# Windowed attention with sink keys and a gated layer behind it: a new order of the vector engine's work, and the sinks and the bias in groups of 32 rows

## The chip, the cores and the metric

The kernel runs on one core of a Trainium2 chip. Times are device microseconds (us) of one execution. The kernel before takes 119.67 us, the median of 3 runs (118.62 to 120.17).

## The reference, cut to what matters

Four batches of 8 heads, 768 positions, 64 values per head. A query sees the 128 keys up to its own position and the 4 first keys of its batch (the sinks). The heads of a position, side by side, make a row of 512 values, which goes through a gated layer.

```python
scores = scale * np.matmul(q, k.transpose(0, 1, 3, 2))
is_sink = pos[None, :] < int(n_sink)                 # n_sink 4
in_window = (rel >= 0) & (rel < int(window))         # window 128, rel = query - key
scores = np.where(is_sink | in_window, scores, -1000000000.0)
a = np.exp(scores - max); a = a / (np.sum(a) + 1e-09)
x = rows of np.matmul(a, v)                          # 3072 rows of 512
H = np.maximum(x @ w_h, 0.0)
T = 1.0 / (1.0 + np.exp(-(x @ w_t + b_t)))
out = T * H + (1.0 - T) * x
```

## The kernel before, in words

The 3072 rows are 24 tiles of 128, 6 for each batch; n is a tile, t its number in the batch. A tile of keys is seen by the queries of its own tile and of the next one, so `scores(n)` multiplies tile n's keys with the queries of tiles n and n+1 (16 matmuls, 4 heads at a time in 4 groups of 32 rows). A tile goes through these functions:

- TensorE (PE): `scores`, `sink_scores` (for t of 2 and more, where the sinks lie outside the window), `values` (exponentials times V, with a first matmul for the sinks' V in each half), `x_transpose`, `bias` (a row of ones times the bias, which starts the sum), `gate` (times w_t), `hidden` (times w_h).
- ScalarE (ACT): `expo` (exponentials of `scores`, into E), `sink_expo`, `x_copy` (the transposed X out of PSUM), `tanh`, and below tile 16 `gate_on_act` (tanh into the gate's value).
- VectorE (DVE): `mask` (E times a mask of zeros and ones), `norm` (a reciprocal of the sums, then X = values times it), `diff` (max(H,0) - X), `gated` (times the gate), and `transpose_qk` or `transpose_tile`, which transpose 32x32 blocks of the loaded Q and K into `tr`.
- GpSimd (POOL): `finish` (adds X, writes O; SP then stores it), `gate_value` from tile 16 on, `sink_keys`, `sink_values`, and nearly all loads: `load_part` (Q and K of batches 0 to 2, a number of neighbouring rows to a partition), `load_whole` (batch 3), `load_v` and `load_v_heads`.

The order on each engine is the order in which the code is written (`_keep_traced_order`). One pass of the loop over s (lines 552 to 599) works on four tiles at once: scores and exponentials of n2 = s+2, mask, values and X of n1 = s+1, gate and hidden of n0 = s, and diff, gated and finish of n9 = s-1. Below, "step n2" is that pass. The lists `pieces`, `tiles` and `loads` say which transposes and loads belong to a step; a load stands ahead of the step's finish on POOL in `loads[n2][0]`, or behind it in `loads[n2][1]`.

In a step DVE's order is diff(n9), mask(n1), gated(n9), the transposes, norm(n1). PE's order is sink_scores(n2), x_transpose(n0), scores(n2), bias(n0), half of gate(n0), values(n1), the other half of gate(n0), hidden(n0). `ps_v` holds the values of a tile, and its second bank X transposed; `ps_z` holds the sink scores and then the gate's sum.

Ahead of the loop (lines 175 to 550) the first tiles are started while the loads come in. SP loads the bias (`b32`, one row) and the sinks' V (`vs32`, 32 rows: head and sink). `sink_values(b)` spreads `vs32` over a block-diagonal `vs[b]`, in POOL's order behind the first loads and ahead of those of batch 1 (`second`).

Of the kernel before, what the change touches and what calls it, by code (L numbers as in the profile page):

```python
# [32 lines left out]
def kernel(  # L33
# [13 lines left out]
    P = 128  # L47
# [59 lines left out]
    def load_part(b, i, g, which, into=None, engine=pool):  # L107

        t0, nt = segments[b][which][i]
        into = nat[b][which][i] if into is None else into  # L110
        engine.dma_start(  # L111
            out=into[32 * g:32 * g + 32].rearrange("p hg m d -> p hg (m d)"),
            in_=(q, k)[which][b, :, t0:t0 + nt, :].rearrange(
                "(g hg) (r m) d -> g r hg (m d)", g=G, m=nt // 32)[g])

    def load_whole(g, which):
        pool.dma_start(
            out=whole[32 * g:32 * g + 32, which].rearrange("p hg m d -> p (hg m) d"),
            in_=(q, k)[which][B - 1].rearrange(
                "(g hg) (m r) d -> g r (hg m) d", g=G, r=32)[g])  # L120

    def part_loads(b, i, which):

        return [lambda g=g: load_part(b, i, g, which) for g in range(G)]
# [12 lines left out]
    def transpose_tile(n):  # L137

        b, t = divmod(n, NC)
        dst = tr[b].bitcast(FP32).rearrange("p w hg t e -> p (w hg) (t e)")  # L140
        src = whole.bitcast(FP32).rearrange("p w hg m d -> p (w hg) (m d)")
        dve.transpose(out=dst[:, :, t * P:(t + 1) * P], in_=src[:, :, t * P:(t + 1) * P])
# [6 lines left out]
    def load_v_heads(b, h0, h1):  # L149
        pool.dma_start(  # L150
            out=vt[b][0][:, h0:h1].rearrange("p h t e -> p (h t) e")[:, :, 0:D],
            in_=v[b, h0:h1].rearrange("h (t p) d -> p (h t) d", p=P))
# [8 lines left out]
    wt = const.tile([P, KC, DM], FP16, tag="wt")  # L161
    brow = const.tile([P, DM], FP16, tag="brow")
    b32 = const.tile([1, DM], FP32, tag="b32")
    ones = const.tile([P, P], FP16, tag="ones")
    zeros = const.tile([P, H * (D + 1)], FP16, tag="zeros")
    vs32 = const.tile([H * NSINK, B, D + 1], FP32, tag="vs32")
    vmask = const.tile([H * NSINK, H], FP32, tag="vmask")
    skmask = const.tile([P, HG, H], FP16, tag="skmask")
    vs = [const.tile([P, H, D + 1], FP16, tag=f"vs{b}", name=f"vs{b}") for b in range(B)]

    sk = [const.tile([P, HG, 2, P], FP16, tag=f"sk{b}", name=f"sk{b}") for b in range(B)]
# [8 lines left out]
    sp.dma_start(out=b32, in_=moe_b_t.unsqueeze(0))  # L180
    for b in range(B):
        sp.dma_start(out=vs32[:, b, 0:D],
                     in_=v[b, :, 0:NSINK, :])
# [14 lines left out]
    dve.memset(brow, 0.0)  # L198
    dve.memset(skmask, 0.0)
    for g in range(G):  # L200
        for hg in range(HG):
            h = HG * g + hg
            dve.memset(skmask[32 * g:32 * g + 32, hg, h:h + 1], 1.0)
    for tile_v in [tile_v for of_batch in vt for tile_v in of_batch]:
        dve.memset(tile_v[:, :, :, D:D + 1], 1.0)
    dve.memset(vs32[:, :, D:D + 1], 1.0)
    for i in range(2):
        dve.memset(es[i], 0.0)
    dve.memset(sk[0].rearrange("p hg e x -> p (hg e x)"), 0.0)
    dve.memset(vs[0].rearrange("p h e -> p (h e)"), 0.0)  # L210
    for b in range(1, B):
        act.copy(out=vs[b].rearrange("p h e -> p (h e)"), in_=zeros)
        act.copy(out=sk[b].rearrange("p hg e x -> p (hg e x)"), in_=zeros[:, 0:HG * 2 * P])
# [7 lines left out]
    pool.memset(vmask, 1.0)  # L221
    pool.affine_select(out=vmask, in_=vmask, compare_op=ALU.is_ge, fill=0.0, base=0,
                       pattern=[[-NSINK, H]], channel_multiplier=1)
    pool.affine_select(out=vmask, in_=vmask, compare_op=ALU.is_ge, fill=0.0,
                       base=NSINK - 1, pattern=[[NSINK, H]], channel_multiplier=-1)


    def sink_keys(b, engine=pool):
        for hg in range(HG):
            engine.tensor_tensor(  # L230
                out=sk[b][:, hg, :, 0:H * NSINK].rearrange("p e (h s) -> p e h s", s=NSINK),
# [5 lines left out]
    def sink_values(b):  # L237
        pool.tensor_tensor(
            out=vs[b][0:H * NSINK],
            in0=vs32[:, b].unsqueeze(1).to_broadcast([H * NSINK, H, D + 1]),  # L240
            in1=vmask.unsqueeze(2).to_broadcast([H * NSINK, H, D + 1]), op=ALU.mult)
# [12 lines left out]


    def sink_bank(n):
        return (ps_h if n == 3 else ps_z)[:, 0:P]

    def sink_scores(n):
        b, t = divmod(n, NC)  # L260
        first = True
        for hg in range(HG):
            for e in range(2):
                last = hg == HG - 1 and e == 1
                pe.matmul(sink_bank(n),
                          lhsT=sk[b][:, hg, e],
                          rhs=tr[b][:, 0, hg, t * P:(t + 1) * P, e], start=first, stop=last)
                first = False

    def sink_expo(n):  # L270
        nrow = H * NSINK
        act.activation(out=es[n % 2][0:nrow], in_=sink_bank(n)[0:nrow],
                       func=AF.Exp, bias=ebias[0:nrow], scale=SCALE)
# [24 lines left out]

    def values(n):
        b, t = divmod(n, NC)  # L300
        both = av_of(n)
        for i in range(2):
            if t >= 2:
                pe.matmul(both[:, i], lhsT=es[n % 2],
                          rhs=vs[b][:, HB * i:HB * i + HB, :].rearrange("p h e -> p (h e)"),
                          start=True, stop=False, skip_group_check=True)
# [53 lines left out]
    def bias(n, cols=ALL):  # L360
# [313 lines left out]
```

## Time and profile before

| | |
|---|---|
| time, median of 3 runs | 119.67 us (118.62, 119.67, 120.17) |
| the profiled execution | 119.51 us |
| its span, first to last instruction | 117.5 us |
| busy: PE, DVE, ACT, POOL | 86%, 83%, 77%, 73% of the span |
| granted TensorE clock, mean | 0.987 |
| DMA packets | 46160, of which 38594 under 512 B |
| `norm` of tile 8, 14, 22 (second instruction) starts at | 50.70, 75.04, 105.94 us |

Busy shares say how full an engine is over the whole span; the order of starts in the timeline says what a step waits for. An instruction's duration and the distance to the next start differ: on DVE and ACT the next one starts some 0.1 us ahead of the recorded end of the one before. Starts are used for sums.

### The profile page before, as it was taken

What the parts mean: (1) busy time and instruction counts of PE and PEld (TensorE: products, weight loads), DVE (VectorE), ACT (ScalarE), POOL (GpSimd) and SP (SyncE); (2) the same over time, 40 slices, a digit from 0 to 9 for tenths busy, and PEclk for the clock granted to TensorE, in tenths of its full rate; (3) what the DMA queues carried; (4) which work ended last, traced back from release to release, by engine and by line L of the source; (5) the groups of instructions that cost most, each with busy time, mean ns of one, the idle gap of its engine ahead of it and who ended that gap; (6) DMA issues with size and microseconds to landing.
All of it is one profiled execution on the core that took longest, in us unless ns stands there. A gap on an engine that the chain in (4) does not pass through costs nothing.

```text
span 117.5 us, 3064 instructions
## 1 busy us (share of the span) xinstructions
PE 101.4 (86%) x1189; PEld 55.8 (48%) x1189; DVE 97.1 (83%) x186; ACT 91.0 (77%) x116; POOL 85.7 (73%) x118
## 2 busy tenths in 40 slices
PE   5997868599969869799999898999998999999920
PEld 1333445345535435556554454655464556555610
DVE  5589875669995899999998999698889998797580
ACT  0985789659769969899699999798788987964510
POOL 6979997499998997798979999530674336415660
PEclk9999999999999999999999999999999999999995
DMA  3999999989999999999999999999310222022032
GB/s 102 238 204 149 140 144 199 147 116 154 106 153 153 284 280 249 182 169 187 206 213 150 198 164 200 154 196 207 108 72 17 89 95 86 3 95 89 27 150 91
DMA packets 46160, 17.52 MB, mean 149 GB/s; under 512 B 38594, under 2 KB 42434, under 8 KB 46147
## 3 DMA queue, kind: packets, MB, share of 16 engines
q0 software_dynamic: 41744, 9.97, 96.9%
q1 hardware_dynamic: 3938, 6.72, 16.8%
q10 hardware_dynamic: 464, 0.66, 2.2%
q8 instruction: 9, 0.15, 0.5%
q14 instruction: 5, 0.03, 0.1%
HBM read 21.01 MB, written 6.29 MB: 232 GB/s over the span
## 4 chain that ended last, share of the span: by engine, by line
PE 38%; DMA 22%; DVE 21%; issue 8%; POOL 4%; ACT 3%; ACTq 1%; DVEq 0%
PE ps_z L365 10%; DMA wh<-in_moe_w_h_dram 9%; PE ps_h L398 9%; DMA nat<-in_k_dram 5%; DVE DD L402 5%; DMA first<-in_q_dram 5%; DVE E L289 5%; DVE tr L134 4%; PE ps_v L316 4%; PE ps_s L250 3%; DVE X L326 3%; DMA nat<-in_q_dram 3%; PE ps_v L313 2%; DVE DD L406 2%; PE ps_v L353 2%
## 5 line engine op out<-in xcount | busy, mean ns | idle before, releaser
L281 ACT ACTIVATE E<-ps_s,ebias 128x2048 f16<-128x2048 f32 (+1 forms) x24 | 43.7, 1822 | 2.1 <-PE ps_s L250 2.1
L411 POOL TENSOR_TENSOR O<-DD,X 128x512 f32<-128x512 f16 (+1 forms) x24 | 27.1, 1134 | 21.4 <-DVE DD L406 13.1
L365 PE MATMUL ps_z<-wt,XT 128*128 128x512 f16 (+1 forms) x96 | 27.6, 375 | 0.4
L398 PE MATMUL ps_h<-wh,XT 128*128 128x512 f16 (+1 forms) x96 | 24.2, 374 | 1.4 <-DMA wh<-in_moe_w_h_dram 1.4
L289 DVE TENSOR_TENSOR E<-E,mask_std 128x2048 f16<-128x2048 f16 (+1 forms) x20 | 22.8, 1138 | 0.3 <-ACT E L281 0.2
L134 DVE STREAM_TRANSPOSE tr<-nat 128x512 f32<-128x512 f32 (+1 forms) x22 | 19.0, 909 | 2.1 <-DMA nat<-in_q_dram 1.1
L402 DVE SCALAR_TENSOR_TENSOR DD<-ps_h,X 128x512 f16<-128x512 f32 (+1 forms) x24 | 16.2, 677 | 4.3 <-PE ps_h L398 3.5
L382 ACT ACTIVATE TH<-ps_z 128x512 f16<-128x512 f32 (+1 forms) x24 | 14.1, 586 | 5.3 <-PE ps_z L365 4.9
L358 ACT COPY XT<-ps_v 128x512 f16<-128x512 f16 x23 | 13.1, 571 | 5.5 <-PE ps_v L353 5.4
L316 PE MATMUL ps_v<-v,E 128*128 128x65 f16 x184 | 15.4, 195 | 1.8 <-DVE E L289 1.5
L326 DVE TENSOR_TENSOR X<-ps_v,rec 128x512 f16<-128x512 f32 x23 | 15.9, 692 | 0.9
L250 PE MATMUL ps_s<-tr 32*128 32x256 f16 (+1 forms) x384 | 14.3, 264 | 1.5 <-DVE mask L492 0.9
L398 PEld LDWEIGHTS <-XT 128*128 128x128 f16 x100 | 9.7, 98 | 11.8 <-issue 1.5
L316 PEld LDWEIGHTS <-E 128*128 128x128 f16 x192 | 12.2, 97 | 6.4 <-DVE E L289 5.1
L313 PE MATMUL ps_v<-v,E 128*128 128x65 f16 x152 | 15.0, 193 | 0.1
L111 POOL DMA_DIRECT2D nat<-in_k_dram x24 | 13.4, 571 | 0.6 <-DMA nat<-in_k_dram 0.6
L313 PEld LDWEIGHTS <-E 128*128 128x128 f16 x160 | 12.5, 98 | 2.3 <-issue 0.2
L111 POOL DMA_DIRECT2D nat<-in_q_dram x20 | 11.2, 564 | 2.2 <-DMA wh<-in_moe_w_h_dram 1.5
L353 PE MATMUL ps_v<-ident,X 128*128 128x128 f16 x92 | 9.0, 220 | 4.2 <-DVE X L326 4.0
L388 ACT ACTIVATE TH<-TH,half 128x512 f16<-128x512 f16 (+1 forms) x17 | 12.0, 709 | 0.5
L191 PE MATMUL ps_h<-zeros 128*128 128x512 f16 x36 | 10.4, 444 | 1.3 <-DVE zeros L194 1.3
L406 DVE TENSOR_TENSOR DD<-DD,TH 128x512 f16<-128x512 f16 (+1 forms) x24 | 10.4, 433 | 0.5 <-POOL TH L393 0.3
(75 smaller groups left out, 131.2 us busy)
## 6 DMA issues: line engine op xcount, KB each, us to landing
out_dram<-O SPq DMA_DIRECT2D x23, 256.0 KB, 5.1
nat<-in_q_dram POOLq DMA_DIRECT2D x16, 96.0 KB, 6.6
nat<-in_k_dram POOLq DMA_DIRECT2D x16, 96.0 KB, 5.5
v<-in_v_dram POOLq DMA_DIRECT2D x4, 384.0 KB, 9.4
v<-in_v_dram POOLq DMA_DIRECT2D x6, 128.0 KB, 5.3
v<-in_v_dram POOLq DMA_DIRECT2D x1, 768.0 KB, 10.8
whole<-in_q_dram POOLq DMA_DIRECT2D x4, 192.0 KB, 6.4
whole<-in_k_dram POOLq DMA_DIRECT2D x4, 192.0 KB, 7.8
```

Source lines behind the costliest of these rows:

```text
L111: engine.dma_start(out=into[32 * g:32 * g + 32].rearrange("p hg m d -> p hg (m d)"), in_=(q, k)[which][b, :, t0:t0 + nt, :].rearrange("(g ...
L134: dve.transpose(out=dst[:, :, lo:hi, :], in_=nat[b][which][i].bitcast(FP32)[:, :, lo:hi, :])
L250: pe.matmul(ps_s[:, g, hg, 0:nq * P], lhsT=tr[b][rows, 1, hg, c * P:(c + 1) * P, e], rhs=tr[b][rows, 0, hg, c * P:(c + nq) * P, e], start= ...
L281: act.activation(out=E[n][:, :, :, 0:nq * P], in_=ps_s[:, :, :, 0:nq * P], func=AF.Exp, bias=ebias, scale=SCALE)
L289: return dve.tensor_tensor(out=e3, in0=e3, in1=m[:, 0:nq * P].unsqueeze(1).to_broadcast([P, H, nq * P]), op=ALU.mult)
L313: pe.matmul(slot, lhsT=E[n - 1][:, g, hg, P:2 * P], rhs=v_of(n - 1)[:, h, :], start=first, stop=False, skip_group_check=True)
L316: pe.matmul(slot, lhsT=E[n][:, g, hg, 0:P], rhs=v_of(n)[:, h, :], start=first, stop=True, skip_group_check=True)
L326: dve.tensor_tensor(out=X[n], in0=av[:, :, :, 0:D], in1=rec.unsqueeze(3).to_broadcast([P, 2, HB, D]), op=ALU.mult)
L365: pe.matmul(z_of(n, cols), lhsT=XT[n][:, kc * P:(kc + 1) * P], rhs=wt[:, kc, cols], start=False, stop=(kc == KC - 1))
L398: pe.matmul(h_of(n, cols), lhsT=XT[n][:, kc * P:(kc + 1) * P], rhs=wh[:, kc, cols], start=(kc == 0), stop=(kc == KC - 1))
L402: dve.scalar_tensor_tensor(out=DD[n][:, cols], in0=h_of(n, cols), scalar=0.0, in1=flat(X[n])[:, cols], op0=ALU.max, op1=ALU.subtract)
L411: ins = pool.tensor_tensor(out=O[n][:, cols], in0=DD[n][:, cols], in1=flat(X[n])[:, cols], op=ALU.add)
```

## The change

Six things are changed.

1. **DVE's order in a step** is mask(n1), diff(n9), gated(n9), norm(n1), transposes. Loads of step 9 and later that stood behind the finish now stand ahead of it, and the first load of a step waits for the step's mask (`behind`).
2. **Sink scores once a batch.** `sinks(b)` runs at t = 2 for tiles 2 to 5 together: 16 matmuls of 32 columns, tile 2+i into partitions 32i to 32i+31 of `ps_z`, and one exponential over 128 partitions in place of four over 32.
3. **Groups of 32 rows.** The sinks' V of a tile are multiplied from 32 rows of `es` and `vs` (`values_of_sinks`), and stand ahead of `gate`, right behind `bias`, which takes one row of another group. For that `vs32` is needed on all 128 partitions: after its four loads SP copies it within SBUF to partitions 32 to 63, and that to 64 to 127. The bias is loaded four times, to rows 0, 32, 64 and 96. The fills with zeros ahead of the loop change with it: six copies on ACT and four memsets on DVE go, others come.
4. **Batch 3 in runs of 2.** `load_whole` takes two neighbouring rows of Q or K (512 B) where it took one (256 B). `transpose_tiles` transposes Q or K of two tiles at a time, writing every second element, in place of Q and K of one tile written densely; there are six such transposes, in steps 15 to 20 rather than 16 to 21.
5. **Loads.** V of tile 4 is issued among the loads of batch 1, ahead of its K, V of tile 5 right behind them. The loads of batches 2 and 3 are spread otherwise over steps 7 to 16.
6. The wait in `finish` becomes the helper `behind`, with no change in what it does.

```diff
-    def load_whole(g, which):
-        pool.dma_start(
-            out=whole[32 * g:32 * g + 32, which].rearrange("p hg m d -> p (hg m) d"),
+    def load_whole(g, which, after=None):
+        behind(pool.dma_start(
+            out=whole[32 * g:32 * g + 32, which].rearrange("p hg (m a) d -> p (hg m) (a d)",
+                                                           a=2),
             in_=(q, k)[which][B - 1].rearrange(
-                "(g hg) (m r) d -> g r (hg m) d", g=G, r=32)[g])
+                "(g hg) (m r a) d -> g r (hg m) (a d)", g=G, r=32, a=2)[g]), after)
...
+    def transpose_tiles(which, t0, t1):
+        dst = tr[B - 1].bitcast(FP32).rearrange("p w hg t e -> p w hg (t e)")[:, which]
+        src = whole.bitcast(FP32)[:, which]
+        dve.transpose(
+            out=dst[:, :, t0 * P:t1 * P].rearrange("p hg (m r a) -> p hg m a r", r=32, a=2),
+            in_=src[:, :, 4 * t0:4 * t1].rearrange("p hg (m a) d -> p hg m a d", a=2))
...
+    for i in range(G):
+        dve.memset(ones_g[32 * i:32 * i + 1, :], 1.0)
+    dve.memset(b32, 0.0)
+    for i in range(G):
+        sp.dma_start(out=b32[32 * i:32 * i + 1, :], in_=moe_b_t.unsqueeze(0))
...
+    dve.memset(vs32.rearrange("p b e -> p (b e)"), 0.0)
...
+    dve.memset(sk.rearrange("p b hg e x -> p (b hg e x)"), 0.0)
+    for b in range(B):
+        sp.dma_start(out=vs32[0:H * NSINK, b, 0:D], in_=v[b, :, 0:NSINK, :])
+    sp.dma_start(out=vs32[32:64], in_=vs32[0:32])
+    sp.dma_start(out=vs32[64:128], in_=vs32[0:64])
...
+    def sink_scores(b):
         first = True
         for hg in range(HG):
             for e in range(2):
+                for i in range(G):
+                    t = 2 + i
+                    pe.matmul(ps_z[32 * i:32 * i + 32, 0:P], lhsT=sk[:, b, hg, e],
+                              rhs=tr[b][:, 0, hg, t * P:(t + 1) * P, e],
+                              start=first, stop=(hg == HG - 1 and e == 1))
                 first = False
...
+    def values_of_sinks(n):
+        b, t = divmod(n, NC)
+        if t >= 2:
+            rows = slice(32 * (t - 2), 32 * (t - 1))
+            for i in range(2):
+                pe.matmul(av_of(n)[:, i], lhsT=es[b % 2][rows],
+                          rhs=vs[b][rows, HB * i:HB * i + HB, :].rearrange("p h e -> p (h e)"),
+                          start=True, stop=False, skip_group_check=True)
...
-    tiles = {n: [n + 2] for n in range(RUNS * NC - 2, N - 2)}
+    tiles = {n: [] for n in range(N)}
+    tiles.update({15: [(0, 0, 2)], 16: [(0, 2, 4)], 17: [(1, 0, 2)], 18: [(0, 4, 6)],
+                  19: [(1, 2, 4)], 20: [(1, 4, 6)]})
...
-    put(segment_loads(2, 0), ((6, 1, 2), (7, 1, 5), (8, 1, 1)))
-    put(v_halves(2), ((8, 1, 1), (9, 1, 1)))
-    put(segment_loads(2, 1), ((8, 1, 1), (9, 1, 2), (10, 1, 5)))
-    put([lambda which=which, g=g: load_whole(g, which)
-         for which in range(2) for g in range(G)], ((11, 1, 3), (12, 1, 3), (13, 1, 2)))
-    put(v_halves(3), ((13, 1, 1), (14, 1, 1)))
+    put(segment_loads(2, 0), ((6, 1, 2), (7, 1, 4), (8, 1, 2)))
+    put(v_halves(2), ((8, 1, 1), (9, 0, 1)))
+    put(segment_loads(2, 1), ((9, 0, 2), (10, 0, 3), (11, 0, 3)))
+    put([lambda after=None, which=which, g=g: load_whole(g, which, after)
+         for which in range(2) for g in range(G)], ((11, 0, 1), (12, 0, 2), (13, 0, 2),
+                                                    (14, 0, 3)))
+    put(v_halves(3), ((15, 0, 1), (16, 0, 1)))
...
     second = segment_loads(1, 0)
+    second.insert(4, lambda: load_v(4))
+    second.append(lambda: load_v(5))
...
         if n2 > 4:
-            if n2 % NC >= 2:
-                sink_scores(n2)
-                sink_expo(n2)
+            if n2 % NC == 2:
+                sinks(n2 // NC)
             x_transpose(n0)
             x_copy(n0)
             scores(n2)
-        bias(n0)
-        if n2 > 4:
+            bias(n0, group=(n1 % NC + 1) % G)
+            values_of_sinks(n1)
             expo(n2)
+        else:
+            bias(n0)
         gate_value(n9)
+        masked = mask(n1) if n2 > 4 else None
         diff(n9)
...
-        else:
-            mask(n1)
         last = gated(n9)
-        for load in loads[n2][0]:
-            load()
+        for i, load in enumerate(loads[n2][0]):
+            load(after=masked if i == 0 else None)
         for n in finished.get(n2, (n9,)):
             finish(n, after=last if n2 < 7 else None)
         for load in loads[n2][1]:
             load()
         if n2 > 4:
+            outputs(n0)
+            gate(n0, parts=range(0, 2))
+            values(n1)
+            norm(n1)
             for piece in pieces[n2]:
                 transpose_qk(*piece)
-        for n in tiles.get(n2, ()):
-            transpose_tile(n)
+        for part in tiles[n2]:
+            transpose_tiles(*part)
         if n2 >= NC and n2 % NC == 0:
             sink_keys(n2 // NC)
         if n2 == N - 1:
             finish(n9, after=mask(n2))
-        if n2 > 4:
-            outputs(n0)
-            gate(n0, parts=range(0, 2))
-            values(n1)
-            norm(n1)
```

## The prediction

> **What bounds the kernel now.** I read the page first: span, busy shares, the row of DMA. The profiled execution took 119.51 us, 1.99 around its span of 117.52; the median is 119.67, so sums against the one hold for the other within 0.2.
>
> ```profile
> span 117.5 us, 3064 instructions
> PE 101.4 (86%) x1189; PEld 55.8 (48%) x1189; DVE 97.1 (83%) x186; ACT 91.0 (77%) x116; POOL 85.7 (73%) x118
> DMA  3999999989999999999999999999310222022032
> ```
>
> No engine stands out, and DMA is full for 28 of 40 slices. So I went on to the timeline of single steps. PE in step 21 (sink scores first):
>
> ```profile
> 94.76 0.39 PE L265 MATMUL ps_z<-tr,sk 128*128 128x128 f16 x4
> 94.99 0.39 PE L353 MATMUL ps_v<-ident,X 128*128 128x128 f16 x4
> 95.31 0.63 PE L250 MATMUL ps_s<-tr 32*128 32x256 f16 x16
> 95.88 0.39 PE L361 MATMUL ps_z<-brow,ones 128*128 128x512 f16 x1
> 96.10 0.59 PE L365 MATMUL ps_z<-wt,XT 128*128 128x512 f16 x2
> 96.53 0.27 PE L304 MATMUL ps_v<-vs,es 128*128 128x260 f16 x1
> 97.43 0.59 PE L365 MATMUL ps_z<-wt,XT 128*128 128x512 f16 x2
> 97.86 1.03 PE L398 MATMUL ps_h<-wh,XT 128*128 128x512 f16 x4
> ```
>
> From start to start: sinks 0.23, transposes 0.32, scores 0.57, bias 0.22, gate 0.43, values 0.90 (of it 0.22 for two sinks' V, and 0.16 in which the second matmul waits for the mask), gate 0.43, hidden 0.91: 4.01 in all. DVE, with three marks of the stages and two waits:
>
> ```profile
> 50.70 0.69 DVE L326 TENSOR_TENSOR X<-ps_v,rec 128x512 f16<-128x512 f32 x1
> ...
> 71.81 1.70 DVE L289 TENSOR_TENSOR E<-E,mask_std 128x2048 f16<-128x2048 f16 x1
> ...
> 75.04 0.69 DVE L326 TENSOR_TENSOR X<-ps_v,rec 128x512 f16<-128x512 f32 x1
> ...
> 94.96 0.69 DVE L402 SCALAR_TENSOR_TENSOR DD<-ps_h,X 128x512 f16<-128x512 f32 x1 [0.26 <-PE ps_h L398]
> 95.57 1.22 DVE L289 TENSOR_TENSOR E<-E,mask_std 128x2048 f16<-128x2048 f16 x1
> 96.70 0.42 DVE L406 TENSOR_TENSOR DD<-DD,TH 128x512 f16<-128x512 f16 x1
> 97.04 0.70 DVE L142 STREAM_TRANSPOSE tr<-whole 128x512 f32<-128x512 f32 x1
> 97.70 0.21 DVE L325 RECIPROCAL rec<-ps_v 128x8 f32<-128x8 f32 x1
> 97.94 0.69 DVE L326 TENSOR_TENSOR X<-ps_v,rec 128x512 f16<-128x512 f32 x1
> 98.92 0.69 DVE L402 SCALAR_TENSOR_TENSOR DD<-ps_h,X 128x512 f16<-128x512 f32 x1 [0.29 <-PE ps_h L398]
> ...
> 105.94 0.69 DVE L326 TENSOR_TENSOR X<-ps_v,rec 128x512 f16<-128x512 f32 x1
> ```
>
> DVE needs 0.61 for diff, 1.13 mask, 0.34 gated, 0.66 transpose, 0.93 reciprocal and X: 3.67, and then waits 0.29 for `hidden`. With the transposes of batches 1 and 2 (0.93 from start to start, as at 53.59) it needs 3.83 to 3.94 and hardly waits. ACT, below tile 16, needs 0.25 for a sink exponential, 0.47 copy, 1.9 expo, 0.63 tanh, 0.63 gate: 3.9. So three engines stand within 0.2 of each other, each behind the others' ends; PE is longest at the end, DVE in the middle. To 45 us the loads decide: K of batch 1 lands at 45.15, its transpose starts at 45.27.
>
> **Part by part.** Marks: X of tiles 8, 14 and 22.
>
> *Sink scores.* ACT loses 12 of 16 small exponentials, 3.0 us. For 16 matmuls of 32 columns there is no row. Between 0.22 (four at a time, 4 x 0.055, the spacing at L265) and 0.88 (one by one) I take the spacing of the 32-row scores, 0.57/16, so 0.57 for 4 x 0.23: PE gains 0.35 a batch. The exponential now stands only in steps 8, 14 and 20; but there PE begins with `sinks`, which needs all queries of the batch: in step 8, those transposed last in step 7.
>
> *Bias and sinks' V.* If two groups of rows run beside each other as scores do, 0.22 goes in each step with t of 2 and more; between 0 and 0.22 I take 0.22, since 16 scores of 256 columns end in 0.57, and one by one, at half of a 512-column bias each, would need 1.76. PE's step falls from 4.01 to 4.01 - 0.23 - 0.22 - 0.16 = 3.40.
>
> *Mask first, X ahead of the transposes.* No work goes; the mask no longer stands behind diff, which waits for `hidden`, and X comes 0.66 to 0.93 earlier in DVE's turn. What is late next is the transposes: keys transposed last in steps 8, 11, 14, 17 and 19 are wanted by PE's scores at the head of the next step. With PE at 3.40 and DVE at 3.83 PE can give that 0.4 a step. So a step costs what DVE needs.
>
> *To tile 8.* I put the new order on the rows from 37.78 on. Step 7: mask 6 at once (E ready at 37.30), diff at 38.9, X at 39.9 rather than 42.32, queries' transposes 41.0 to 42.5. Step 8: sinks behind them, PE's transposes of X at 43.1 (before, behind X's end at 43.0); X of tile 7 at 45.4, key transposes 46.2 to 47.7. Step 9: X of tile 8 at 50.0. Gain **0.7**.
>
> *Tiles 8 to 14.* Five steps at 3.83 and one with half a mask (0.60 for 1.13) at 3.3: 22.5 where 24.34 were. Against it POOL: in steps 9 to 14 two to four loads now stand between mask and finish, 0.54 each for Q and K (L111), 1.43 for half of V, 0.93 for `whole`. The finish (1.15) is clear of the next mask if the loads need less than 3.83 - 1.25 - 1.15 = 1.43. Steps 9 (2.5), 11 (2.5) and 14 (2.8) are over that by an us. What such a meeting costs is the 1.70 at 71.81, beside this finish:
>
> ```profile
> 71.25 1.17 POOL L411 TENSOR_TENSOR O<-DD,X 128x512 f32<-128x512 f16 x1
> ```
>
> It is 0.48 over the usual 1.22 for 0.61 beside each other. Between 0 and 1.15 a meeting I take this row: 3 x 0.48 = 1.4. Gain 24.34 - 22.5 - 1.4 = **0.4**. The Trainium skill (SBUF — State Buffer, section "Who interferes with whom") says that a VectorE instruction with two SBUF inputs and a GpSimd one that reads SBUF shut each other out for the whole instruction, whoever issues first. By that the three meetings would be some 1.0 each, an estimate, this gain -1.2 and the time 118.4; the mechanism stands below as rival C, from rows.
>
> *Tiles 14 to 22.* The transposes of batch 3 write every second element: between 0.66 (L142, dense) and 0.93 (L134, every eighth or twelfth); by the step I take nearer the first, 0.75. A step with one needs 3.76, less 0.06 of reciprocal that no longer waits: 3.70; one with half a mask, or none to transpose, goes with PE at 3.4. X 15 to 22: 5 x 3.70 + 3 x 3.4 = 28.7, and 0.5 for `gate_value` (0.62), which can now meet the mask in steps 19 to 23, for one row like 71.81. 29.2 where 30.90 were: gain **1.7**. At 0.66 it is 2.1, at 0.93 it is 0.8.
>
> *Loads.* V of tile 4 goes 2.1 us forward on POOL, K of batch 1 0.9 back; that K (29.02 now) is wanted behind X of tile 4, at 32. `whole` in 512 B rows halves 12288 packets; K of batch 3, ready 0.6 ahead of use now (77.20, 77.80), is wanted one step later. No gain taken.
>
> *Ahead of the loop.* DVE's fills grow by 0.65 us and end near 4.95; the first K cast waits until 5.28. ACT's six copies (4.10 to 7.3) go, but it waits for Q until 7.74. `vs32` is the danger: by the trace's DMA semaphores its four loads, issued from 4.22 on, were complete at 9.79 to 11.02. They now stand behind four bias rows (a queue's DMA starts behind the landing of its eighth predecessor: Q at 18.55 behind wt's 18.27), so issue from 6.4 to 9.3 and land near 12.8; then two copies, one behind the other. Each between 2.0 (a store at 90.90) and 5.6 (the first vs32 load): `vs32` at 16.8 to 24; I take 3.2 each, 19. POOL reaches `sink_values(0)` at 15.61 and would idle, with the loads of batch 1 behind it; but its third waits until 22.68 for wh's landing, and V of tile 3 lands at 24.86. Cost 0.0 to 0.3, in the 0.7 above already.
>
> *Tail.* Behind X 22 nothing moves but 32-row sinks' V, which here have no bias beside them: +0.1.
>
> **Sum:** 119.5 - 0.7 - 0.4 - 1.7 + 0.1 = **116.8**.
>
> **Rivals.**
>
> *A. More of it.* No meetings, transposes dense (0.66): 116.8 - 1.4 - 0.4 = 115.0. For it: only one mask of 20 now shows a long meeting. Against: the finish moved toward the mask.
>
> *B. The row groups don't run side by side.* Bias and sinks' V cost what they did, `sinks` 0.88; PE at 3.7 decides where DVE had 3.4 (tiles 17, 21, 22) and eats the slack of the others: +0.3 x 3, +0.05 x 10: 118.2. For it: one matmul with one row isn't a score. The Trainium skill (TensorEngine Tiling (Array Packing), section "Key Properties") says a change of tiling mode drains TensorE; the row is XT ahead of scores, 0.32 where four matmuls of 128 columns take 0.23. The change adds two such changes a batch.
>
> *C. POOL and DVE in lockstep.* The mask waits for the finish, the finish for the loads, the loads for the mask: a step lasts 1.25 + loads + 1.15. Steps 9, 10, 11, 12 (with sink_keys 0.55), 13, 14: 4.9, 4.0, 4.9, 4.3, 4.3, 5.2 for 3.83 (12: 3.3), so 5.1 over, where I count 1.4: 120.5. It decides from loads of 1.43 on. Against: if the mask starts first, the finish waits instead, and nothing behind that is urgent.
>
> *D. `vs32` too late* (the slower side). Two copies at 5.6 give 24. Then sinks' values to 26.7, four Q loads to 29.9, landing at 31.9 rather than 26.53; DVE's transpose at 26.66 waits, with all behind it: +5.4 on the forecast, 122.2. Slower than before from an arrival at about 21.5 on. Against: small transfers of 8 KB landed 0.2 to 0.6 apart.
>
> **How the numbers follow.** Forecast 0.40 (own range 115.8 to 117.9), A 0.30, B 0.10, C 0.11, D 0.09. A measurement of this kernel tells about 2% from no change: 117.3 and 122.1. Faster: A, three quarters of the forecast and a little of B: 0.61. Slower: half of D and a tail of C: 0.08. Same: 0.31. The range reaches from A's lower part, 114.2, to where C and D begin to be left out, 120.3.
>
> **What would show it.** Right: in step 21 of the new profile no wait of L316 for the mask, bias and sinks' V within 0.3 together, DVE without a wait for `hidden`; X of tile 8 near 50, tile 14 near 74, tile 22 near 103. Transposes of `whole` near 0.8. Wrong: masks of 1.7 and more in steps 10 to 15 (C), a POOL gap over 4 us ahead of the first `sink_values` (D), bias and sinks' V 0.44 apart (B), DVE waiting for nat or whole (then the loads pace the kernel, and none of the sums hold).

## The result, and the profile after

The change made the kernel **slower**: a median of 128.67 us (127.64 to 129.20, 4 runs) against 119.15 us (118.56 to 120.17, 4 runs) of the kernel before on the same chip, a ratio of 1.078 (95% interval 1.067 to 1.089). That is 11.9 us more than the forecast of 116.8. Ratios here, also below, leave out executions that took over 1.5% more than the fastest of the same kernel, so a median can stand a little off its ratio.

The page of the changed kernel first: the span, what each engine did in it, and the DMA engines' share in 40 slices.

```profile
span 125.9 us, 3063 instructions
...
PE 100.4 (80%) x1189; PEld 50.5 (40%) x1189; DVE 104.2 (83%) x189; ACT 85.4 (68%) x98; POOL 88.5 (70%) x118
...
DMA  3999999136999999999999999989932012220242
```

ACT lost 5.6 us of work, as meant, and DVE gained 7.1, which nobody meant. In the row of DMA there is a hole at slices 8 and 9 (22 to 28 us) that the kernel before doesn't have. Line numbers are now those of the changed kernel: L303 is the mask, L423 diff, L427 gated, L344 and L345 the reciprocal and X, L144 and L151 the transposes, L254 the sinks' values, L432 the finish, L414 `gate_value`, L318 the sinks' V on PE.

The hole has its cause in the chain of work that ended last (start, us, what). Two copies of `vs32` from SBUF to SBUF stand in it, one behind the other:

```profile
11.78 6.93 DMA vs<-vs
18.73 4.81 DMA vs<-vs
```

The timelines of POOL and of DVE (start, length, engine, line, operation, idle time before it and its releaser) show who waits for them:

```profile
23.77 2.08 POOL L254 TENSOR_TENSOR vs<-vs,vmask 128x520 f16<-128x520 f32 x2 [8.17 <-DMA vs<-vs]
...
26.57 0.21 DVE L344 RECIPROCAL rec<-ps_v 128x8 f32<-128x8 f32 x1 [6.81 <-PE ps_v L335]
```

POOL stands 8.17 us at `sink_values(0)`, with the loads of Q of batch 1 queued behind it (they land at 28.5 to 31.4 where they landed at 25.1 to 26.5). PE needs these values for tile 2, and DVE waits 6.81 for PE. X of tile 2 starts at 26.82 rather than 21.34.

The loop has another loss. Two steps on DVE, and POOL's finishes in the same time:

```profile
79.00 1.80 DVE L303 TENSOR_TENSOR E<-E,mask_std 128x2048 f16<-128x2048 f16 x1
80.72 0.68 DVE L423 SCALAR_TENSOR_TENSOR DD<-ps_h,X 128x512 f16<-128x512 f32 x1
81.50 0.43 DVE L427 TENSOR_TENSOR DD<-DD,TH 128x512 f16<-128x512 f16 x1
81.84 0.20 DVE L344 RECIPROCAL rec<-ps_v 128x8 f32<-128x8 f32 x1
82.08 0.69 DVE L345 TENSOR_TENSOR X<-ps_v,rec 128x512 f16<-128x512 f32 x1
82.69 0.70 DVE L151 STREAM_TRANSPOSE tr<-whole 128x512 f32<-128x512 f32 x1
83.31 2.04 DVE L303 TENSOR_TENSOR E<-E,mask_std 128x2048 f16<-128x2048 f16 x1
```

```profile
78.53 1.17 POOL L432 TENSOR_TENSOR O<-DD,X 128x512 f32<-128x512 f16 x1
...
83.09 1.17 POOL L432 TENSOR_TENSOR O<-DD,X 128x512 f32<-128x512 f16 x1
```

Each of these masks begins while a finish runs. The finishes end at 79.70 and 84.26, the masks at 80.80 and 85.35: 1.10 and 1.09 behind the finish. A mask that meets a running finish thus ends as if it did nothing until POOL is done and then took its 1.09. And diff (80.72) to gated (81.50) is 0.78 from start to start, though diff lasts 0.68: in the steps shown of before, diff to mask was 0.61 and mask to gated 1.13, with no gap. The groups of instructions (busy us, mean ns of one, idle before them) have both losses in sum:

```profile
L303 DVE TENSOR_TENSOR E<-E,mask_std 128x2048 f16<-128x2048 f16 (+1 forms) x20 | 27.9, 1396 | 0.2 <-ACT E L295 0.2
...
L427 DVE TENSOR_TENSOR DD<-DD,TH 128x512 f16<-128x512 f16 (+1 forms) x24 | 10.6, 442 | 2.6 <-POOL TH L414 0.5
```

The same two groups before:

```profile
L289 DVE TENSOR_TENSOR E<-E,mask_std 128x2048 f16<-128x2048 f16 (+1 forms) x20 | 22.8, 1138 | 0.3 <-ACT E L281 0.2
...
L406 DVE TENSOR_TENSOR DD<-DD,TH 128x512 f16<-128x512 f16 (+1 forms) x24 | 10.4, 433 | 0.5 <-POOL TH L393 0.3
```

### The profile page after: what moved, and what is told of

It reads as the page before. It is cut to its first block, busy times and chain, and to the rows that moved or that the text cites. A ratio compares the mean times of both kernels' runs of the same rounds, so it can differ in the third digit from the quotient of the medians.

```text
span 125.9 us, 3063 instructions
## 1 busy us (share of the span) xinstructions
PE 100.4 (80%) x1189; PEld 50.5 (40%) x1189; DVE 104.2 (83%) x189; ACT 85.4 (68%) x98; POOL 88.5 (70%) x118
## 4 chain that ended last, share of the span: by engine, by line
DVE 29%; PE 28%; ACT 14%; DMA 12%; issue 10%; POOL 3%; SPq 1%; DVEq 0%; POOLq 0%; ACTq 0%
DVE E L303 11%; DMA vs<-vs 9%; PE ps_z L386 7%; DVE tr L144 6%; ACT E L295 6%; PE ps_h L419 6%; PE ps_v L335 4%; PE ps_s L265 3%; ACT TH L403 3%; DVE X L345 3%; ACT XT L377 3%; DMA vs<-in_v_dram 2%; PE ps_v L332 2%; DVE DD L423 2%; ACT TH L409 2%
## 5 line engine op out<-in xcount | busy, mean ns | idle before, releaser
L432 POOL TENSOR_TENSOR O<-DD,X 128x512 f32<-128x512 f16 (+1 forms) x24 | 28.3, 1181 | 16.2 <-DVE DD L427 8.1
L303 DVE TENSOR_TENSOR E<-E,mask_std 128x2048 f16<-128x2048 f16 (+1 forms) x20 | 27.9, 1396 | 0.2 <-ACT E L295 0.2
L419 PE MATMUL ps_h<-wh,XT 128*128 128x512 f16 (+1 forms) x96 | 25.1, 385 | 0.0
L144 DVE STREAM_TRANSPOSE tr<-nat 128x512 f32<-128x512 f32 (+1 forms) x22 | 18.9, 904 | 0.6 <-DMA nat<-in_q_dram 0.4
L423 DVE SCALAR_TENSOR_TENSOR DD<-ps_h,X 128x512 f16<-128x512 f32 (+1 forms) x24 | 16.0, 665 | 1.0 <-PE ps_h L419 1.0
L345 DVE TENSOR_TENSOR X<-ps_v,rec 128x512 f16<-128x512 f32 x23 | 15.9, 691 | 0.8
L335 PE MATMUL ps_v<-v,E 128*128 128x65 f16 x184 | 14.1, 197 | 2.2 <-DVE E L303 1.8
L335 PEld LDWEIGHTS <-E 128*128 128x128 f16 x192 | 12.1, 98 | 7.6 <-DVE E L303 6.5
L332 PE MATMUL ps_v<-v,E 128*128 128x65 f16 x152 | 13.4, 196 | 0.1
L332 PEld LDWEIGHTS <-E 128*128 128x128 f16 x160 | 11.6, 100 | 3.0 <-issue 1.1
L427 DVE TENSOR_TENSOR DD<-DD,TH 128x512 f16<-128x512 f16 (+1 forms) x24 | 10.6, 442 | 2.6 <-POOL TH L414 0.5
L344 DVE RECIPROCAL rec<-ps_v 128x8 f32<-128x8 f32 x23 | 4.6, 201 | 9.4 <-PE ps_v L335 9.1
L265 PEld LDWEIGHTS <-tr 32*128 32x128 f16 x384 | 7.5, 93 | 11.3 <-DVE tr L144 6.0
```

Source lines behind the costliest of these rows:

```text
L144: dve.transpose(out=dst[:, :, lo:hi, :], in_=nat[b][which][i].bitcast(FP32)[:, :, lo:hi, :])
L265: pe.matmul(ps_s[:, g, hg, 0:nq * P], lhsT=tr[b][rows, 1, hg, c * P:(c + 1) * P, e], rhs=tr[b][rows, 0, hg, c * P:(c + nq) * P, e], start= ...
L303: return dve.tensor_tensor(out=e3, in0=e3, in1=m[:, 0:nq * P].unsqueeze(1).to_broadcast([P, H, nq * P]), op=ALU.mult)
L332: pe.matmul(slot, lhsT=E[n - 1][:, g, hg, P:2 * P], rhs=v_of(n - 1)[:, h, :], start=first, stop=False, skip_group_check=True)
L335: pe.matmul(slot, lhsT=E[n][:, g, hg, 0:P], rhs=v_of(n)[:, h, :], start=first, stop=True, skip_group_check=True)
L345: dve.tensor_tensor(out=X[n], in0=av[:, :, :, 0:D], in1=rec.unsqueeze(3).to_broadcast([P, 2, HB, D]), op=ALU.mult)
```

## The experiments

The theory after this comparison: three losses, namely the copies (4 to 5 us), the order with the mask first (the gap of 0.17 in each step, and more meetings), and the finish behind the loads. Each was undone alone, then all three. In each diff `-` is the changed kernel.

**Straight loads.**

```
-    for b in range(B):
-        sp.dma_start(out=vs32[0:H * NSINK, b, 0:D], in_=v[b, :, 0:NSINK, :])
-    sp.dma_start(out=vs32[32:64], in_=vs32[0:32])
-    sp.dma_start(out=vs32[64:128], in_=vs32[0:64])
+    for b in range(B):
+        for i in range(G):
+            sp.dma_start(out=vs32[32 * i:32 * i + 32, b, 0:D], in_=v[b, :, 0:NSINK, :])
```

> Sink values of V loaded from DRAM straight into all four groups of 32 partitions, 16 small loads on SP and no copy from SBUF to SBUF; all else as changed. Theory (the two copies, 6.93 and 4.81 us, hold POOL at sink_values(0) for 8.17 us, and the loads of batch 1 behind it are late, which costs some 4 to 5 us at tile 2 and is never given back): X of tile 2 starts near 21.5 for 26.82, POOL's wait ahead of L254 falls from 8.2 to under 3, and the time falls by 4 to 5, to 123 to 125. Rival 1 (the late stretch is absorbed later, because the loads of the next batches decide the steps to tile 8 anyway): X of tile 2 comes earlier, X of tile 8 does not, the time stays within 1 us of 128.7. Rival 2 (the chain is the whole loss): the time falls to 119 or below.

Measured: median 125.43, ratio 1.045 (1.034 to 1.057), which is 3.3% less than the change, or some 4 us. POOL's wait is 2.0. But X of tile 2 starts at 24.38, not 21.5, and the two timelines name what took the place of the stall (line numbers are one lower here; the profiled execution is the longest of the four, 126.14):

```profile
14.99 2.67 DVE L302 TENSOR_TENSOR E<-E,mask_std 128x2048 f16<-128x2048 f16 x1
...
15.49 1.08 POOL L253 TENSOR_TENSOR vs<-vs,vmask 128x520 f16<-128x520 f32 x1
```

The mask of tile 1 took 2.67 for 1.22 and again ended 1.09 behind POOL's product (16.57); with all three edits (below) it took 2.71 at the same place. PE's granted clock was down as well, to 0.52 and 0.62 in the stretches from 20 to 24 us. The theory's place was right; the time just missed its 123 to 125, as a second wait appeared.

**Mask second.**

```
-        masked = mask(n1) if n2 > 4 else None
         diff(n9)
+        masked = mask(n1) if n2 > 4 else None
```

> In the steps of the loop the mask stands between diff and gated again, as before the change; all else as changed. Theory (with nothing between them, gated waits for the end of diff, 0.78 from start to start where diff to mask and mask to gated leave no gap, about 0.17 a step in 19 steps; and the mask, going first, stands more often beside POOL's finish, sink_keys and gate_value): the masks' mean falls from 1396 ns to under 1300, the time falls by 3 to 6, to 123 to 126. Rival (mask first is a gain as forecast, since the mask doesn't stand behind hidden, and the losses come from elsewhere): the time rises by 1 to 2 us, steps of the end go from 3.64 back to 4.0.

Measured: 129.13, ratio 1.082 (1.072 to 1.092): no gain. This part of the theory fell. The masks did get shorter (mean 1224 ns) and the gap closed (idle ahead of gated 0.5), but the time came back in front of the reciprocal, which in the changed kernel had 9.4 us of idle time ahead of it:

```profile
L344 DVE RECIPROCAL rec<-ps_v 128x8 f32<-128x8 f32 x23 | 4.7, 206 | 17.9 <-PE ps_v L335 16.4 <-ACT E L295 0.9 <-ACT TH L409 0.6
```

With X ahead of the transposes nothing but gated stands between the mask's end and X, and PE's values, which need the mask, aren't done by then. In this order X first is only to be had with the mask first.

**Finish first.**

```
-        for i, load in enumerate(loads[n2][0]):
-            load(after=masked if i == 0 else None)
         for n in finished.get(n2, (n9,)):
             finish(n, after=last if n2 < 7 else None)
-        for load in loads[n2][1]:
+        for load in loads[n2][0] + loads[n2][1]:
             load()
```

> The finish goes ahead of all loads of its step on POOL, and no load waits for the mask; all else as changed. Theory (in the steps of tiles 8 to 14 the loads push the finish beside the next mask, masks of 1.88, 1.80 and 2.04 us for 1.21): tiles 8 to 14 take about 24 for 26.18 and the time falls by 2 to 3, to 126; the masks beside gate_value and the slow sink_keys stay. Rival 1 (the masks are long because they come first, whichever of POOL's instructions is beside them): the meetings move to other steps, masks' mean within 50 ns of 1396, time within 1 us of 128.7. Rival 2 (lockstep is the whole loss in the middle): the time falls by 4 or more.

Measured: 125.22, ratio 1.048 (1.038 to 1.057), 3.0% better than the change; masks' mean 1214 ns. Tiles 8 to 14 took 24.24 for 26.18, as expected, and tiles 14 to 22 took 30.77 for 31.75. From tile 9 on the masks of the changed kernel are 5.3 us longer than they need, in ten of them; here 1.9, all in tiles 17 to 22. The rival (they are long because they come first) falls.

**All three.** The three edits above together.

> All three edits together: straight loads of the sinks' V, mask between diff and gated, finish ahead of the loads. Theory (chain, order of the mask and late finish are the three losses, about 4.5, 4 and 1.5 with the last two overlapping): 117 to 119.5, level with the kernel before. Rival (something else in the change costs as well, transposes behind X or the sinks at the head of PE's turn): 121 or more.

Measured: 125.53, ratio 1.049 (1.043 to 1.056). The rival held in time. Mask second showed a likely reason: it costs what it gives, and with the finish first there are fewer long masks for it to shorten. In the profile tiles 8 to 14 take 25.75 where finish first alone has 24.24, and X of tile 2 is at 25.40, behind the mask of 2.71 and with a granted clock of 0.50 to 0.52 from 18 to 24 us.

**The beginning mended.** Straight loads, finish first, mask first, and the sinks' values of batches 0 and 1 on DVE, behind masks 1 and 2.

```
+    sink_values(0, engine=dve)      # ahead of norm(1)
...
+    sink_values(1, engine=dve)      # ahead of norm(2)
```

> As the kernel with straight loads of the sinks' V, and with the finish ahead of the loads; besides, the sinks' values of batches 0 and 1 are made by DVE, in its waits ahead of X of tiles 1 and 2, and not by POOL beside mask 1, which took 2.67 us there with straight loads alone. Theory (the start costs 5.4 us at tile 8 in two parts, the copies and POOL's 128-row product beside the mask, and the late finish 2.5 to 3.4 in the loop; nothing else is large): mask 1 at 1.22, X of tile 2 near 21.9, X of tile 8 near 51.0, the loop as with the finish first (24.2 for tiles 8 to 14, 30.8 from there to 22), time 119.5 to 120.5, level with the kernel before. Rival (something else in the first 25 us is late as well, the sinks' scores of all tiles at the head of PE's turn or the clock): X of tile 2 at 23 or later, time over 121.5.

Measured: 122.87, ratio 1.025 (1.016 to 1.033). Mask 1 is 1.22, but X of tile 2 comes at 23.71: the rival. In this profile PE's granted clock was down to 0.6 and 0.7 in the two slices from 18 to 24 us. The next two kernels have the same beginning and a clock of 1.00 there, and X of tile 2 at 22.71 and 22.63: so about 1.0 of the delay goes with the clock, and 1.3 is there without it.

**Three orders.** On that beginning, first the gap covered (the transposes go from behind X to between diff and gated), with POOL kept off the masks:

```
         masked = mask(n1) if n2 > 4 else None
         diff(n9)
+        if n2 > 4:
+            for piece in pieces[n2]:
+                transpose_qk(*piece)
+        for part in tiles[n2]:
+            transpose_tiles(*part)
...
-        for n in finished.get(n2, (n9,)):
-            finish(n, after=last if n2 < 7 else None)
+        for n in finished.get(n2, (n9 - 1,)):
+            finish(n, after=last if n2 < 7 else masked)
...
-        return n < 16 or n == N - 1       # on_act
+        return True
```

> As the kernel with the mended start, but a step's transposes stand between diff and gated, X comes behind gated, the finish of a tile waits for the next step's mask, and the gate's half-and-shift is on ACT for all tiles. Theory (between diff and gated DVE stands 0.17 when nothing is put there; the masks are long only beside POOL's work): a step with 0.93 of transposes goes from 4.02 to 3.85, masks' mean under 1200, tiles 8 to 14 in 23.3, tiles 14 to 22 in 29.5, time 117 to 118.5. Rival (PE or ACT take over at 3.7 to 3.9 a step, or the finish beside diff and transposes makes these longer): 119 to 121.

Measured: 120.42 for the profiled execution and 122.48 to 123.00 for the other three, a median of 122.63 without an interval; so the time decides nothing here beyond that the 117 to 118.5 of the theory was not reached. In the one profile, tiles 8 to 14 took 22.59 and 14 to 22 30.02, the first better than expected, the second worse. But X of tile 7 took 6.46: the sink scores of tile 8 waited 2.7 us for `sink_keys(1)`, which the late finishes of tiles 0 to 3 had pushed back on POOL.

Then, on the same beginning, DVE's order of the kernel before (diff, mask, gated, transposes, X):

> As the kernel with the mended start, but DVE's order in a step is that of the kernel before: diff, mask, gated, transposes, X. So of the change only sink scores at once, the groups of 32 rows, the last batch's runs of 2 and the loads are left. Theory (DVE's turn needs 3.87 again, as before, and bounds the step; PE's and ACT's savings are cover): the loop as before, 24.3 and 30.9, time within 1 us of 119.7. Rival (PE's 0.35 and 0.22 a step and ACT's 3 us come through, since hidden is done earlier and diff waits less): 117 to 118.5.

Measured: 119.55, ratio 0.999 (0.995 to 1.004). The theory held in the time; the loop took 23.36 and 30.74, an us better than before in its first part, and the beginning had X of tile 2 1.3 late. Sink scores at once, the groups of rows, the runs of 2 and the later loads together are worth nothing that shows in the time, although they take 5 us from ACT and some work out of PE's step. The theory's reason, that DVE's own turn bounds the step, fits tiles 8 to 14, but not the end: from tile 14 on diff still waits 0.24 to 0.36 for `hidden` in most steps. There a step is a ring through two engines: mask at 79.83, the first matmul of values that needs it at 81.10, the second half of gate at 81.58, `hidden` at 82.01, diff at 83.14, and the next mask at 83.75, 3.92 later. The sink scores, the bias and the sinks' V stand outside that ring, so what they save doesn't shorten this step.

And the other way round, the kernel before with the mask ahead of diff alone:

> The kernel before with the mask ahead of diff and nothing else of the change; X stays behind the transposes. Theory (0.17 more between diff and gated in some 19 steps, against up to 0.29 of waiting for hidden that goes in the steps of the end; the masks meet gate_value more often): between 119.5 and 122.5, no gain. Rival (the mask first is the gain that was forecast): 118 or less.

Measured: 119.98, ratio 1.002 (0.997 to 1.006). Diff's wait for `hidden` falls from 3.5 us to 1.0, and the gap ahead of gated grows from 0.5 to 2.6; masks' mean goes from 1138 to 1249. What mask first gives, it takes.

**Both orders.** The old order up to X of tile 7, the covered one behind it; then the same with `gate_value` left on POOL.

> The mended start; to the step that makes X of tile 7 DVE's order of the kernel before, with the finish in its place; from there on mask, diff, transposes, gated, X, with the finish behind the next step's mask and the gate's half-and-shift on ACT for all tiles. Theory (the order mask first is worth something once the gap behind diff is filled and POOL is kept off the masks: the covered kernel needed 52.6 us from X of tile 8 to X of tile 22 where the kernel before needs 55.2, and the old order has X of tile 8 at 50.9): X of tile 22 at 103.5, time 116.5 to 117.8, faster than both kernels. Rival (the covered loop only caught up on slack that its late start left in loads and ACT): X 8 to 22 in 54 or more, time 118.5 to 120.

> As the kernel with both, but the gate's half-and-shift of tiles 16 to 22 stays on POOL, where it meets the masks of the last steps. Theory (a meeting costs DVE at least what POOL's instruction lasts): masks of 1.4 to 1.6 in the last steps, 0.5 to 1.5 us slower than the kernel with both, 117.5 to 119. Rival (PE bounds the last steps at 3.65, so that long masks there are hidden): within 0.3 us of it or faster.

Measured: 119.58, ratio 0.998 (0.992 to 1.003), and 119.28, 1.001 (0.997 to 1.004). The time that the theory expected, faster than both kernels, did not come. The loop is as the theory had it: X of tile 8 to X of tile 22 in 52.77 where the kernel before needs 55.24. It was lost ahead of the loop: X of tile 2 at 23.82 for 21.34, with the granted clock again at 0.50 from 20 to 22 us. With the gate on POOL the masks are longer (mean 1182 for 1109 ns) and the same stretch takes 53.44, yet the times don't differ: there the theory of 0.5 to 1.5 us more was not borne out.

**The beginning once more.** The sinks' values of batch 0 behind mask 2 and of batch 1 behind the first gated product, in waits of DVE; with and without four idle matmuls on PE.

```
-    sink_values(0, engine=dve)      # ahead of norm(1)
     norm(1)
+    keep_warm(4)                    # in the first of the two kernels only
...
+    sink_values(0, engine=dve)      # behind mask(2)
     values_of_sinks(2)
     values(2)
-    sink_values(1, engine=dve)
...
     gated(0)
+    sink_values(1, engine=dve)
```

> As the kernel with both, but sinks' values of batch 0 are made behind mask 2 and those of batch 1 behind the first gated product, so that X of tiles 1 and 2 doesn't wait for them; and four idle matmuls (0.2 us each) stand on PE behind the values of tile 1, where the kernel before has the sink scores of tile 3. Theory (the start is late by 1.1 to 1.5 at tile 8 because of 0.4 of sinks' values ahead of X 1, and because PE, idle for 1.5 to 2 us at 17, gets half its clock from 18 to 23): clock at 1.00 from 18 to 24, X of tile 2 at 21.8 to 22.2, X of tile 8 at 50.9, X of tile 22 at 103.6, time 117.0 to 118.2, faster than before by 1 to 2 us. Rival (the dip comes whatever PE does there, or the loads of batch 1 set X of tile 8): X of tile 8 at 51.5 or later, 119.

> The same without the four idle matmuls. Theory (the granted clock falls when PE has been idle there): clock at 0.5 in some 2 us between 18 and 24, X of tile 2 1 to 1.5 later than with them, time 0.3 to 1.3 more. Rival (the wait is only that of sinks' values, which are moved): no difference between the two.

Measured: 118.08, ratio **0.989 (0.984 to 0.994)**, and 118.84, 0.988 (0.982 to 0.995). Both are about 1.1% faster than the kernel before, a small gain, but its interval lies clear of 1. X of tile 2 is at 21.30 and 21.54, X of tile 8 at 50.79 in the first. The idle matmuls made no difference, and the clock was at 1.00 from 16 to 30 us with them and without: that part of the theory fell. How much of the gain is the new place of the sinks' values, and how much a clock that didn't fall in these two profiles, isn't separated. A step of the first one on DVE has no gap and no long mask:

```profile
51.39 1.22 DVE L302 TENSOR_TENSOR E<-E,mask_std 128x2048 f16<-128x2048 f16 x1
52.53 0.69 DVE L422 SCALAR_TENSOR_TENSOR DD<-ps_h,X 128x512 f16<-128x512 f32 x1
53.13 1.09 DVE L144 STREAM_TRANSPOSE tr<-nat 128x512 f32<-128x512 f32 x1
54.06 0.41 DVE L426 TENSOR_TENSOR DD<-DD,TH 128x512 f16<-128x512 f16 x1
54.39 0.19 DVE L343 RECIPROCAL rec<-ps_v 128x8 f32<-128x8 f32 x1
54.62 0.69 DVE L344 TENSOR_TENSOR X<-ps_v,rec 128x512 f16<-128x512 f32 x1
55.22 1.22 DVE L302 TENSOR_TENSOR E<-E,mask_std 128x2048 f16<-128x2048 f16 x1
```

From mask to mask it is 3.83, the very figure that the forecast had for the changed kernel, where its steps from tile 9 to 14 took 4.01 to 4.70.

**The price of the beginning.** The mended loop with the changed kernel's beginning put back, first whole, then with straight loads.

> The best kernel so far (the idle matmuls behind tile 1), but with the whole beginning of the changed kernel put back: the sinks' V copied twice from SBUF to SBUF, their values made on POOL ahead of the loads of batch 1, no idle matmuls. The loop stays mended. Theory (the beginning alone costs 4 to 5.3 us, and none of it comes back, since DVE bounds every later step): X of tile 8 near 55.5 to 56, time 122 to 123.5. Rival (the loop makes up for a late beginning, as its loads are then ahead of need): 120.5 or less.

> The same with the sinks' V loaded straight from DRAM, values still on POOL, where the first product of 128 rows stands beside mask 1. Theory (of the beginning's cost the copies are 2.5 to 3, and POOL's product beside the mask and the idle PE behind it are the other 2): mask 1 at 2.6, X of tile 8 near 52.5 to 53.5, time 119.5 to 121. Rival (the copies are the whole cost): X of tile 8 at 51, time 118.

Measured: 123.36, ratio 1.035 (1.029 to 1.041), and 119.50, 0.992 (0.985 to 1.000). The two differ by the copies alone: 4.3% of the kernel before, 5.1 us, by the two intervals about 1 more or less. Hardly any of it comes back: with the whole old beginning X of tile 8 is 6.4 behind the best kernel's (57.15 for 50.79), X of tile 22 still 5.8 (109.80 for 104.03). The first theory held in the time, though X of tile 8 came an us later than it had. The second had the copies at only 2.5 to 3; its rival, that they are the whole cost, comes closer, since in time the rest can't be told from nothing (0.992 against 0.989), though the profile with straight loads has X of tile 8 at 52.45. The mask of tile 1 took 1.22 this time and POOL's product beside it was the longer one (1.39 for 1.05), but the mask of tile 2 (18.88) met the next product (18.79, 1.05 long) and took 2.05.

## Why the prediction was wrong

By its own marks, in the traces (us; the best is the kernel with the four idle matmuls):

| | before | forecast | changed | finish first | best |
|---|---|---|---|---|---|
| to X of tile 8 | 50.70 | 50.0 | 55.90 | 56.08 | 50.79 |
| X 8 to X 14 | 24.34 | 23.94 | 26.18 | 24.24 | 23.24 |
| X 14 to X 22 | 30.90 | 29.2 | 31.75 | 30.77 | 30.00 |

*To tile 8: missed by 5.9, the largest term.* The step that failed is "I take 3.2 each, 19" for the two copies. They took 6.93 and 4.81, where the same sentence named 5.6 as the upper bound of one, and `vs32` was whole at 23.54, inside its range of 16.8 to 24. So "Cost 0.0 to 0.3" was 5.1 by the last two experiments. The argument against rival D, that small transfers landed 0.2 to 0.6 apart, spoke of loads side by side, and these two stand one behind the other. D's mechanism and price were near the mark: four loads of Q held up behind POOL landed by 31.44 (it had 31.9), the transpose of 26.66 started at 31.56, and the 5.4 was 5.1. It didn't have the other wait, which comes first: DVE stands 6.81 at X of tile 2 for PE's values. The one arrival seen lies beyond D's point of decision of 21.5, which is all that can be said of it. Its chance of 0.09 rested on the argument that fails; the upper third of the forecast's own range for `vs32` was already beyond that point. Both signs that were named for C and D came: a POOL gap of 8.17, and masks of 1.88 and 1.80 in steps 11 and 15.

*Tiles 8 to 14: missed by 2.24.* "3 x 0.48 = 1.4" for meetings: they cost 2.3 by the masks' lengths. The count of three was right, the price was not: the masks of tiles 10, 11 and 14 were 0.66, 0.99 and 0.58 longer. The mask at 71.81 of before follows the same rule (its finish ended at 72.42, the mask 1.09 later), but a meeting costs about what is left of the finish when the mask starts, and that was 0.61 there and 0.70 to 1.10 here. One of the three wasn't where it was forecast: the finish of step 9, beside the mask at 57.44, took 2.21, and the next one, so delayed, met the mask of tile 10: in part rival C, whose lockstep I had argued away with "the finish waits instead". About 1.0 is the gap of 0.17 in six steps, which no step of the prediction has: it summed starts of another order, in which the mask covers what gated waits for. Some 0.3 is left, of it 0.18 in a longer gated beside that late finish.

*Tiles 14 to 22: missed by 2.55.* `gate_value` and `sink_values(3)` and the finishes together lengthened seven masks by some 3.1 us where 0.5 stood; the gap takes 1.4 more. Against it, the transposes in runs of 2 go at 0.62 from start to start, where dense ones took 0.63 to 0.66 before and I took 0.75: 0.8 on the good side. That comes to 3.2, 0.65 more than the miss. By the starts the difference lies in the three steps that the forecast gave to PE at 3.4 (X of tiles 17, 21 and 22): DVE had slack there, and part of its longer work went into it.

*What was right.* `hidden` no longer holds DVE up. ACT's load fell by more than the 3.0 counted. Of the 16 matmuls of 32 columns, 15 took 0.34 (48.54 to 48.88) where I took 0.57 for all. The groups of rows do run side by side, against rival B; PE in a step with sinks' V:

```profile
66.53 0.64 PE L265 MATMUL ps_s<-tr 32*128 32x256 f16 x16 [0.60 <-DVE tr L144]
67.00 0.38 PE L382 MATMUL ps_z<-brow,ones_g 1*128 1x512 f16 x1
67.01 0.38 PE L318 MATMUL ps_v<-vs,es 32*128 32x260 f16 x2
67.32 0.60 PE L386 MATMUL ps_z<-wt,XT 128*128 128x512 f16 x2
```

Bias and sinks' V start 0.01 apart, and from scores to gate it is 0.79 where 0.57 + 0.22 + 0.22 = 1.01 stood: the 0.22 forecast. But this is so in four of the eleven such steps from tile 8 to 22. In the other seven the sinks' V start later than the bias and scores to gate takes 1.05 to 1.38; for instance they wait for the copy of X's transpose, which shares their bank (107.77 to 108.36, the sinks' V from 108.41), and the 0.22 is lost. Step 21, which the prediction named for its sign of 0.3, is one of these: bias to gate is 0.51. And old order on the mended beginning shows that PE's gain is worth nothing in the time when it lies outside what bounds the step.

In sum: of the 11.9 us, the copies cost 5.1, and the changed loop against the mended one, on the same beginning, 4.3% (1.078 less 1.035) or some 5.1 more, of which the finish behind the loads is 3.0%. Even the best kernel is 1.3 above the forecast: its marks are 0.8 late at tile 8 and 0.8 slow from tile 14 to 22.

## What to carry to other kernels

Price a serial chain of transfers by the longest row there is, and ask what is queued behind its first reader; here some 100 KB of copies stopped POOL, and with it the next batch's loads. Before moving an instruction forward, look at what it covered where it stood: a wait of 0.17 between two dependent neighbours came out from under the mask and took back what the move gave. Where two engines shut each other out, place the second one's work by the first one's turn (finish behind the mask), not by when its data are ready.

## What was not expected of the hardware

- *The mask and POOL's element-wise work shut each other out.* In eleven meetings of the changed kernel a whole mask ended 1.07 to 1.10 behind POOL's instruction, whether that was a finish, `gate_value` or the sinks' product; two masks of half the width ended 0.55 and 0.56 behind it. The Trainium skill (SBUF — State Buffer, section "Who interferes with whom") says that they shut each other out for the whole instruction; these rows agree. Where the mask began first, POOL's instruction was mostly the longer one (the two of `sink_keys` 1.56 at 70.84 for 0.55), but with straight loads alone the mask at 14.99, begun 0.5 ahead of POOL's product, waited for it all the same; who goes first isn't settled by the recorded starts.
- POOL's DMA issues do no such thing: with the finish first, masks wholly beside them took 1.20 (77.84) and 1.18 (81.55).
- A copy of 32.5 KB from SBUF to SBUF took 6.93 us while the row of DMA stood at 9, and one twice as large took 4.81 behind it, as the loads ran out.
- Two dependent instructions in turn on DVE start 0.78 apart where an independent one could have started at 0.61.
- PE's granted clock fell behind the long stall (0.67 from 24 to 26 us, 0.50 from 26 to 28), and to 0.50 in some of the kernels with straight loads as well (20 to 22 us), not in others with the same beginning. The idle matmuls didn't tell why. The Trainium skill (TensorE: Matmul & The Clock Gate, section "Part 1: The HAM clock gate") says that the clock is halved after an idle window of about 3.4 us, and that these windows run freely, whatever the kernel does; the halves and the differing runs of one beginning agree with that. An idle window is seen only in the long stall, though: in the kernel with both orders PE was busy for 1.27 and 1.11 of the 2 us stretches ahead of the fall (16 to 20 us). No run here shows the windows, so it stays open.
